# Moving the top-k penalty from VectorE's comparison to ScalarE's Sign in a fused attention and SwiGLU kernel

## The chip, the core and the metric

The kernel runs on one core of one Trainium2 chip. The metric is the device time of one execution in microseconds (us). In what follows PE is TensorE (PEld its weight load), DVE is VectorE, ACT is ScalarE, POOL is GpSimd, SP is SyncE, which issues most of the transfers.

## What is computed

Attention over 8 batches, 8 heads, 576 positions and 64 dimensions, in which each query keeps its 32 largest scores, followed by a SwiGLU block on the 4608 x 512 result:

```python
scores = scale * np.matmul(q, k.transpose(0, 1, 3, 2))
kth = np.partition(scores, -top_k, axis=-1)[..., -top_k:-top_k + 1]
scores = np.where(scores >= kth, scores, -1000000000.0)
scores = scores - np.max(scores, axis=-1, keepdims=True)
attn = np.exp(scores)
attn = attn / (np.sum(attn, axis=-1, keepdims=True) + 1e-09)
out = np.matmul(attn, v)
# x = out as (B*S, H*D)
g = x @ w_gate
silu = g * (1.0 / (1.0 + np.exp(-g)))
result = (silu * (x @ w_val)) @ w_out
```

The feed-forward width is 1536. All data are fp32.

## The kernel before

The work on attention is cut into 160 **units**: a batch, a tile of queries and a pair of heads. Of each batch's five tiles four have 128 queries (two heads side by side, 1152 score columns: a full unit), the last has 64 (both heads share the partitions, 576 columns). The feed-forward part is cut into 18 blocks of 256 rows of x, and each block into 36 **pieces** of four matmul calls; a call appears as two matmuls in the profile. The loop spreads pieces among the units. The weights are rounded once, in 72 pieces of 128x256, on ScalarE, GpSimd and VectorE, while the first units run.

The 32 largest of each row are found on VectorE in four rounds of eight; then VectorE compares the scores with the 32nd largest, and GpSimd adds the penalty:

```python
def select(n):
    ...
    e = work.tile([P, 2 * S], FP32, tag="e", name="e", bufs=4)
    for r in range(rounds):
        for t, hs in enumerate(heads):
            nc.vector.max(m[:, t, 8 * r : 8 * r + 8], cur[:, hs])          # L271
            yield
        if r < rounds - 1:
            for t, hs in enumerate(heads):
                nc.vector.match_replace(...)                               # L275
                yield
            cur = rest
    for t, hs in enumerate(heads):
        nc.vector.tensor_scalar(                                           # L281
            e[:, hs], sc[:, hs], m[:, t, TOP_K - 1 : TOP_K], FAR, ALU.is_lt, ALU.mult
        )

def penalize(n):
    nc.gpsimd.tensor_scalar_mul(bias[:, 0:nh], m[:, 0:nh, 0], -scale)      # L291
    nc.gpsimd.tensor_tensor(e[:, every], e[:, every], sc[:, every], ALU.add)   # L293

def weigh(n):           # ScalarE: Exp with the row sum                      L302
def normalize(n):       # GpSimd: + EPS L312; VectorE: reciprocal L314; ScalarE: scale L317
def turn(n):            # TensorE transposes e (L329), ScalarE copies the banks to et (L330)
def values(n):          # TensorE: et by v (L349, L358), ScalarE copies to xT (L373)
def scores(n):          # TensorE: L250 (L236 in the short tile), ScalarE copies to sc (L255, L241)
```

The score banks, the transposed banks, av and the banks of key and query preparation come from one pool of five PSUM tiles (`ps_t`); the products of the feed-forward block from another of three (`ps_f`).

A block of the feed-forward part; `need` drains the rounding of weights until those that the next product reads are there:

```python
def need(n):
    while ready[0] < n:
        next(weight)

def product(w, s, then):
    ps = ps_f.tile([P, 2, BLK], FP32, tag="f", name="f")
    need(8 * s + (4 if w is wg else 8))
    for i in range(2):
        m = 2 * s + i
        for kc in range(KC):
            nc.tensor.matmul(ps[:, i, :], w[:, kc, m * P : (m + 1) * P], x[:, kc, :], ...)  # L412
        if i == 1:
            on_act.append(lambda: then(ps))
        yield
# gate: Tanh (L430), half of g (L431), + 1 (L432) on ScalarE, then h * half on GpSimd (L433)
# value: copy on ScalarE (L437), then h * val on GpSimd (L438)
# output: matmuls of h by w_out (L449), copy on ScalarE (L460), store
```

One pass of the loop, cut:

```python
    flush(on_act)                     # ScalarE's part of the last products
    next(norm, None)                  # GpSimd: tot + EPS of unit n - 2
    penalize(n - 1)
    flush(on_pool)
    run(turn(n - TURN))               # TURN = 3
    finish_unit(n - VALUES)           # VALUES = 4
    next(nxt, None)                   # TensorE: scores of unit n + 1
    weigh(n - 1)                      # ScalarE: Exp of unit n - 1
    run(nxt)                          # ScalarE: copies to sc
    dve(2, beside=False)              # four steps of select(n)
    pieces(2); flush(on_act); flush(on_pool)
    dve(1); dve(1); next(norm, None); run(norm)
    next(ahead, None); pieces(1); next(ahead, None)
    dve(1); pieces(1); dve(2); run(topk); pieces(6)
```

`dve` also advances the rounding of the weights, about 4.5 of its pieces per full unit. Each engine runs its instructions in the order in which they are written here.

Of the kernel before, what the change touches and what calls it, by code (L numbers as in the profile page):

```python
# [8 lines left out]
AF = mybir.ActivationFunctionType  # L9
ALU = mybir.AluOpType  # L10
# [5 lines left out]
P = 128  # L16
TOP_K = 32
LOWEST = -3.4028234663852886e38
FAR = -3.0e38
EPS = 1.0e-9  # L20
BLK = 256
WP = 256
# [5 lines left out]
def kernel(  # L28
# [7 lines left out]
    w_out: bass.AP,  # L36
    out: bass.AP,
):

# [102 lines left out]
        for _ in range(n):  # L144
            next(weight, None)

    def need(n):

        while ready[0] < n:
            next(weight)  # L150

    pairs = [(b, hp) for b in range(B) for hp in range(NHP)]
    raw, preps = {}, {}
# [66 lines left out]
    def scores(n):  # L220
        b, qt, hp = units[n]
        slab = preps[b * NHP + hp]
        sc = work.tile([P, 2 * S], FP32, tag="sc", name="sc", bufs=2)
        halves = [slice(0, D), slice(D, P)]
        half = S // 2

        def bank():
            return ps_t.tile([P, 512], FP32, tag="t", name="s")


        if qt == J:
            banks = [bank() for _ in range(2)]
            for i, ps in enumerate(banks):
                for d in halves:
                    k0 = R + i * half
                    nc.tensor.matmul(  # L236
                        ps[d, 0:half], slab[d, S + R : S + 2 * R], slab[d, k0 : k0 + half]
                    )
            yield
            for i, ps in enumerate(banks):  # L240
                nc.scalar.copy(sc[:, i * half : (i + 1) * half], ps[:, 0:half])  # L241
        else:
            q0 = S + 2 * R + qt * P
            banks = []
            for i in range(2):
                for hh, d in enumerate(halves):
                    ps = bank()
                    banks.append((i + 2 * hh, ps))
                    k0 = (1 - hh) * R + i * half
                    nc.tensor.matmul(  # L250
                        ps[:, 0:half], slab[d, q0 : q0 + P], slab[d, k0 : k0 + half]
                    )
            yield
            for i, ps in banks:
                nc.scalar.copy(sc[:, i * half : (i + 1) * half], ps[:, 0:half])  # L255
        state[n] = dict(sc=sc)

    def select(n):

        nh = n_heads(units[n][1])  # L260
        sc = state[n]["sc"]
        m = small.tile([P, 2, TOP_K], FP32, tag="m", name="m", bufs=2)
        heads = [slice(t * S, (t + 1) * S) for t in range(nh)]
        rest = work.tile([P, 2 * S], FP32, tag="rest", name="rest", bufs=1)
        e = work.tile([P, 2 * S], FP32, tag="e", name="e", bufs=4)
        state[n] |= dict(m=m, e=e, heads=heads)
        cur = sc
        rounds = TOP_K // 8
        for r in range(rounds):
# [5 lines that stand above are left out]
                    nc.vector.match_replace(  # L275
                        rest[:, hs], m[:, t, 8 * r : 8 * r + 8], cur[:, hs], LOWEST
                    )
                    yield
                cur = rest
        for t, hs in enumerate(heads):  # L280
            nc.vector.tensor_scalar(  # L281
                e[:, hs], sc[:, hs], m[:, t, TOP_K - 1 : TOP_K], FAR, ALU.is_lt, ALU.mult
            )

    def penalize(n):

        st = state[n]
        sc, m, e, heads = st.pop("sc"), st.pop("m"), st["e"], st["heads"]
        nh = len(heads)
        bias = small.tile([P, 2], FP32, tag="bias", name="bias")  # L290
        nc.gpsimd.tensor_scalar_mul(bias[:, 0:nh], m[:, 0:nh, 0], -scale)  # L291
        every = slice(0, nh * S)
        nc.gpsimd.tensor_tensor(e[:, every], e[:, every], sc[:, every], ALU.add)  # L293
        st["bias"] = bias

    def weigh(n):

        st = state[n]
        e, heads, bias = st["e"], st["heads"], st.pop("bias")
        tot = small.tile([P, 2], FP32, tag="tot", name="tot")  # L300
        for t, hs in enumerate(heads):
            nc.scalar.activation(  # L302
                e[:, hs], e[:, hs], AF.Exp, bias=bias[:, t : t + 1], scale=scale,
                accum_out=tot[:, t : t + 1],
            )
        st["tot"] = tot
# [87 lines left out]
    def flush(queue):  # L394
        while queue:
            queue.pop(0)()

    def feed(kb):

        x = xT.pop(kb)
        hs = []

        def product(w, s, then):
            ps = ps_f.tile([P, 2, BLK], FP32, tag="f", name="f")
            need(8 * s + (4 if w is wg else 8))
            for i in range(2):
                m = 2 * s + i  # L410
                for kc in range(KC):
                    nc.tensor.matmul(  # L412
                        ps[:, i, :],
                        w[:, kc, m * P : (m + 1) * P],
                        x[:, kc, :],
                        start=(kc == 0),
                        stop=(kc == KC - 1),
                    )
                if i == 1:
                    on_act.append(lambda: then(ps))  # L420
                yield

        for s in range(MS):
            h = ffn.tile([P, 2, BLK], FP32, tag="h", name="h", bufs=MS + 1)
            hs.append(h)


            def gate(ps, h=h):
                half = ffn.tile([P, 2, BLK], FP32, tag="gv", name="half_g", bufs=3)
                nc.scalar.activation(h[:], ps[:], AF.Tanh, scale=0.5)  # L430
                nc.scalar.mul(half[:], ps[:], 0.5)  # L431
                nc.scalar.add(h[:], h[:], 1.0)  # L432
                on_pool.append(lambda: nc.gpsimd.tensor_mul(h[:], h[:], half[:]))  # L433

            def value(ps, h=h):
                val = ffn.tile([P, 2, BLK], FP32, tag="gv", name="val", bufs=3)
                nc.scalar.copy(val[:], ps[:])  # L437
                on_pool.append(lambda: nc.gpsimd.tensor_mul(h[:], h[:], val[:]))  # L438

            yield from product(wg, s, gate)  # L440
            yield from product(wv, s, value)
        for t in range(BLK // P):
            ps = ps_f.tile([P, DM], FP32, tag="f", name="o_ps")
            for m in range(MC):
                need(8 * MS + 2 * m + 2)
                if m == 6:
                    flush(on_act)
                    flush(on_pool)
                nc.tensor.matmul(  # L449
                    ps[:],  # L450
                    hs[m // 2][:, m % 2, t * P : (t + 1) * P],
                    wo[:, m, :],
                    start=(m == 0),
                    stop=(m == MC - 1),
                )
                if m == MC - 1:

                    def finish(ps=ps, t=t):
                        o = ffn.tile([P, DM], FP32, tag="o", name="o")
                        nc.scalar.copy(o[:], ps[:])  # L460
                        store(o, kb * BLK + t * P)

                    on_act.append(finish)
                if m % 2 == 1:
                    yield

    NU = len(units)
    todo = list(range(NBLK))
# [2 lines left out]
    def piece():  # L471

        if len(on_act) > 1:
            flush(on_act)
        if len(on_pool) > 1:
            flush(on_pool)
        while True:
            if not current:
                if not todo or done.get(todo[0], 0) < NHP * BLK:
                    return False  # L480
                flush(on_act)
                flush(on_pool)
                current.append(feed(todo.pop(0)))
            if next(current[0], 0) == 0:
                current.pop()
                continue
            return True

    def fetch(n):

# [5 lines left out]
            load(i + NHP)  # L496

    def pieces(n):
        for _ in range(n):
            if credit[0] >= 1 and piece():  # L500
                credit[0] -= 1

    def run(steps):
        for _ in steps:
# [19 lines left out]
    for n in range(NU + VALUES):  # L524
# [7 lines left out]
        def dve(k, beside=True):  # L532

            for _ in range(k * nh):
                next(topk, None)
                due[0] += 5 / 11 if beside else 0
                if due[0] >= 1:
                    due[0] -= 1
                    rounding(1)
# [11 lines left out]
            run(turn(n - TURN))  # L551
        if n >= VALUES:
            finish_unit(n - VALUES)
        next(nxt, None)
        if 0 <= n - 1 < NU:
            weigh(n - 1)
        run(nxt)

        dve(2, beside=False)
# [11 lines left out]
        next(ahead, None)  # L571
        pieces(1)
        next(ahead, None)
        dve(1)
        pieces(1)
        dve(2)
# [52 lines left out]
```

## Time and profile before

| what | value |
|---|---|
| median of 3 runs | 1914.77 us (1911.7 to 1914.82) |
| profiled run | 1915.14 us, span 1913.4 us |
| TensorE busy | 1756.5 us, 92% |
| VectorE busy | 1608.9 us, 84% |
| ScalarE busy | 1156.3 us, 60% |
| GpSimd busy | 816.0 us, 43% |
| mean granted TensorE clock | 0.959 |

The profile page gives the busy time of each engine, the span in 40 slices with the busy share in tenths, the chain of work that ended last, and the costliest groups of instructions with their mean duration and the idle time of the engine ahead of them. The clock row (PEclk) is what the throttle granted, in tenths of full speed. Busy times of TensorE include slow stretches at half clock, so its busy share has to be read together with that row.

### The profile page before, as it was taken

How to read it: one execution, taken by the hardware profiler on the slowest of the kernel's cores; microseconds unless marked ns; L12 is line 12 of the kernel's file. 1: busy time of each engine (PE TensorE's matmuls, PEld its weight loads, DVE VectorE, ACT ScalarE, POOL GpSimd, SP SyncE). 2: the span in 40 equal slices, each digit the busy share in tenths (PEclk: the TensorE clock that was granted, in tenths of full speed). 3: DMA queues.
4: the chain of work that ended last, by engine and by line, in shares of the span. 5: the costliest groups of instructions: out<-in, count | busy, mean ns of one | idle time of the engine just before them, and what ended most of it. 6: DMA issues, size and time to landing. Idle time of an engine off the chain costs nothing.

```text
span 1913.4 us, 29363 instructions
## 1 busy us (share of the span) xinstructions
PE 1756.5 (92%) x10144; PEld 1297.0 (68%) x10144; DVE 1608.9 (84%) x3476; ACT 1156.3 (60%) x2821; POOL 816.0 (43%) x846
## 2 busy tenths in 40 slices
PE   3437789989999999999999999999999999999999
PEld 2336558667677777676768676868686868586866
DVE  7999889998899979998799979999799989999400
ACT  5656656566666656675657566656675656665421
POOL 4566644335343525353335343525243535353412
PEclk7668899989999999999999999999999999999999
DMA  7322202000300012000210003000210001000000
GB/s 185 88 78 82 67 22 69 11 1 3 76 12 12 2 27 63 12 1 13 53 37 1 12 4 87 1 12 1 60 31 12 1 14 45 18 1 12 1 12 11
DMA packets 111253, 59.58 MB, mean 31 GB/s; under 512 B 89088, under 2 KB 97280, under 8 KB 111104
## 3 DMA queue, kind: packets, MB, share of 16 engines
q1 hardware_dynamic: 109904, 57.41, 11.5%
q8 instruction: 80, 1.31, 0.3%
q14 instruction: 69, 0.57, 0.1%
q10 hardware_dynamic: 1200, 0.30, 0.1%
HBM read 48.23 MB, written 9.44 MB: 30 GB/s over the span
## 4 chain that ended last, share of the span: by engine, by line
PE 82%; DVE 6%; POOL 5%; ACT 4%; issue 2%; DMA 0%; SPq 0%; POOLq 0%; DVEq 0%; ACTq 0%
PE f L412 38%; PE o_ps L449 19%; PE av L358 8%; PE etps L329 7%; PE s L250 7%; DVE m L271 2%; POOL e L293 2%; DVE rest L275 2%; PE s L236 2%; ACT e L302 1%; PE av L349 1%; PE kqps L205 1%; ACT sc L255 1%; POOL size L113 1%; POOL size L103 1%
## 5 line engine op out<-in xcount | busy, mean ns | idle before, releaser
L271 DVE MAX8 m<-rest 128x8 f32<-128x576 f32 x864 | 615.2, 747 | 2.2
L275 DVE MATCH_REPLACE8 rest<-m,rest 128x576 f32<-128x576 f32 x576 | 424.1, 743 | 0.0
L412 PE MATMUL f<-xT,wg 128*128 128x256 f32 x1728 | 407.5, 386 | 0.0
L293 POOL TENSOR_TENSOR e<-e,sc 128x1152 f32<-128x1152 f32 (+1 forms) x160 | 382.7, 2392 | 42.4 <-DVE e L281 38.8
L412 PE MATMUL f<-xT,wv 128*128 128x256 f32 x1728 | 395.8, 381 | 0.0
L449 PE MATMUL o_ps<-wo,h 128*128 128x512 f32 x864 | 387.6, 598 | 0.0
L412 PEld LDWEIGHTS f<-xT,wg 128*128 128x128 f32 x1728 | 324.2, 191 | 71.5 <-issue 29.9
L412 PEld LDWEIGHTS f<-xT,wv 128*128 128x128 f32 x1728 | 325.3, 190 | 53.3 <-issue 10.5
L433 POOL TENSOR_TENSOR h<-h,half_g 128x512 f32<-128x512 f32 x108 | 138.4, 1282 | 453.0 <-ACT h L432 435.0
L271 DVE MAX8 m<-sc 128x8 f32<-128x576 f32 x288 | 205.6, 750 | 123.9 <-ACT sc L255 78.8
L329 PE MATMUL etps<-ident,e 128*128 128x128 f32 (+1 forms) x1312 | 187.5, 288 | 125.9 <-POOL size L103 48.1
L449 PEld LDWEIGHTS o_ps<-wo,h 128*128 128x128 f32 x864 | 159.4, 190 | 193.1 <-issue 186.9
L329 PEld LDWEIGHTS etps<-ident,e 128*128 128x128 f32 (+1 forms) x1312 | 159.4, 147 | 176.1 <-POOL size L103 51.3
L330 ACT COPY et<-etps 128x512 f32<-128x512 f32 (+1 forms) x448 | 184.7, 482 | 148.5 <-PE etps L329 147.1
L302 ACT ACTIVATE e<-e,bias 128x576 f32<-128x576 f32 x288 | 222.1, 776 | 74.9 <-POOL e L293 74.5
L317 ACT ACTIVATE e<-e,tot 128x576 f32<-128x576 f32 x288 | 210.5, 780 | 5.4 <-DVE tot L314 5.1
L275 DVE MATCH_REPLACE8 rest<-m,sc 128x576 f32<-128x576 f32 x288 | 211.9, 742 | 0.0
L438 POOL TENSOR_TENSOR h<-h,val 128x512 f32<-128x512 f32 x108 | 139.7, 1293 | 149.6 <-ACT val L437 149.6
L250 PE MATMUL s<-kqT 64*128 64x288 f32 x1024 | 173.1, 446 | 9.6 <-ACT kqT L210 6.4
L312 POOL TENSOR_SCALAR tot<-tot 128x2 f32<-128x2 f32 (+1 forms) x160 | 37.4, 234 | 329.3 <-ACT e L302 320.9
L358 PE MATMUL av<-et,v 128*64 128x128 f32 (+1 forms) x2560 | 174.6, 282 | 0.0
L255 ACT COPY sc<-s 128x288 f32<-128x288 f32 x512 | 165.0, 410 | 2.5 <-PE s L250 2.5
(44 smaller groups left out, 1436.0 us busy)
## 6 DMA issues: line engine op xcount, KB each, us to landing
kq_in<-in_k_dram SPq DMA_DIRECT2D x64, 128.0 KB, 2.8
v<-in_v_dram SPq DMA_DIRECT2D x32, 256.0 KB, 3.0
kq_in<-in_q_dram SPq DMA_DIRECT2D x62, 128.0 KB, 3.1
w<-in_moe_w_gate_dram SPq DMA_DIRECT2D x24, 256.0 KB, 2.7
w<-in_moe_w_val_dram SPq DMA_DIRECT2D x24, 256.0 KB, 2.7
w<-in_moe_w_out_dram SPq DMA_DIRECT2D x24, 256.0 KB, 2.6
out_dram<-o SPq DMA_DIRECT2D x40, 128.0 KB, 2.4
out_dram<-o SPq DMA_DIRECT2D x16, 256.0 KB, 2.3
```

The costliest lines, as they stand in the source:

```text
L250: nc.tensor.matmul(ps[:, 0:half], slab[d, q0 : q0 + P], slab[d, k0 : k0 + half])
L255: nc.scalar.copy(sc[:, i * half : (i + 1) * half], ps[:, 0:half])
L271: nc.vector.max(m[:, t, 8 * r : 8 * r + 8], cur[:, hs])
L275: nc.vector.match_replace(rest[:, hs], m[:, t, 8 * r : 8 * r + 8], cur[:, hs], LOWEST)
L293: nc.gpsimd.tensor_tensor(e[:, every], e[:, every], sc[:, every], ALU.add)
L302: nc.scalar.activation(e[:, hs], e[:, hs], AF.Exp, bias=bias[:, t : t + 1], scale=scale, accum_out=tot[:, t : t + 1],)
L317: nc.scalar.mul(e[:, hs], e[:, hs], tot[:, t : t + 1])
L329: nc.tensor.transpose(ps[0:kl, c * P : (c + 1) * P], e[:, k0 : k0 + kl], ident[:])
L330: nc.scalar.copy(et[0:kl, c0 : c0 + cn, :], ps[0:kl, 0 : cn * P].rearrange("p (c j) -> p c j", c=cn),)
L358: nc.tensor.matmul(av[hh * R : (hh + 1) * R, 0:ql], v_last[:, hh, :] if c == J else vt[:, hh, c, :], moving, start=last and c == 0, stop=c ...
L412: nc.tensor.matmul(ps[:, i, :], w[:, kc, m * P : (m + 1) * P], x[:, kc, :], start=(kc == 0), stop=(kc == KC - 1),)
L449: nc.tensor.matmul(ps[:], hs[m // 2][:, m % 2, t * P : (t + 1) * P], wo[:, m, :], start=(m == 0), stop=(m == MC - 1),)
```

## The change

The comparison goes from VectorE. Instead ScalarE computes the sign of 2^30 x (score - 32nd largest), which is -1, 0 or 1; GpSimd takes the minimum with 0 and multiplies by 3e38, and adds the score, head by head. The negative of the 32nd largest, scaled, is made by a small GpSimd operation (`least`). This is meant to relieve VectorE, which in the first part of the kernel also rounds weights. Exp (`weigh`) moves from ahead of the score copies to after the normalization of the unit before. The tile e is taken in `penalize`, with three buffers instead of four; sc has three instead of two.

The first two feed-forward blocks are computed in halves of 128 rows, so that the first products can start when four units' values are there and not eight. And products no longer force the rounding of weights: where the weights are not there yet, the loop goes on without a piece.

```diff
-        for t, hs in enumerate(heads):
-            nc.vector.tensor_scalar(
-                e[:, hs], sc[:, hs], m[:, t, TOP_K - 1 : TOP_K], FAR, ALU.is_lt, ALU.mult
-            )
 
     def penalize(n):
...
+        e = work.tile([P, 2 * S], FP32, tag="e", name="e", bufs=3)
+        least = small.tile([P, 2], FP32, tag="least", name="least")
+        nc.gpsimd.tensor_scalar_mul(least[:, 0:nh], m[:, 0:nh, TOP_K - 1], -FINE)
         bias = small.tile([P, 2], FP32, tag="bias", name="bias")
         nc.gpsimd.tensor_scalar_mul(bias[:, 0:nh], m[:, 0:nh, 0], -scale)
-        every = slice(0, nh * S)
-        nc.gpsimd.tensor_tensor(e[:, every], e[:, every], sc[:, every], ALU.add)
-        st["bias"] = bias
+        for t, hs in enumerate(heads):
+            nc.scalar.activation(
+                e[:, hs], sc[:, hs], AF.Sign, bias=least[:, t : t + 1], scale=FINE
+            )
+            nc.gpsimd.tensor_scalar(e[:, hs], e[:, hs], 0.0, FAR, ALU.min, ALU.mult)
+            nc.gpsimd.tensor_tensor(e[:, hs], e[:, hs], sc[:, hs], ALU.add)
+        st |= dict(e=e, bias=bias)
...
-    def need(n):
+    def until(n):
         while ready[0] < n:
-            next(weight)
+            yield 0
...
+    def parts(kb):
+        return [slice(0, P), slice(P, BLK)] if kb < 2 else [slice(0, BLK)]
...
-        def product(w, s, then):
+        def product(w, s, c, then):
+            n = c.stop - c.start
+            yield from until(8 * s + (4 if w is wg else 8))
             ps = ps_f.tile([P, 2, BLK], FP32, tag="f", name="f")
-            need(8 * s + (4 if w is wg else 8))
...
-                        ps[:, i, :],
+                        ps[:, i, 0:n],
                         w[:, kc, m * P : (m + 1) * P],
-                        x[:, kc, :],
+                        x[:, kc, c],
...
-                yield
+                yield n / BLK
...
+        for c in parts(kb):
+            while done[kb] < NHP * c.stop:
+                yield 0
...
-        next(nxt, None)
-        if 0 <= n - 1 < NU:
-            weigh(n - 1)
         run(nxt)
...
         next(ahead, None)
         pieces(1)
         next(ahead, None)
+        if 0 <= n - 1 < NU:
+            weigh(n - 1)
         dve(1)
         pieces(1)
```

More of the change, by code (lines that the diff above doesn't have):

```diff
@@ L18 @@
 LOWEST = -3.4028234663852886e38
-FAR = -3.0e38
+FAR = 3.0e38
+FINE = 2.0**30
 EPS = 1.0e-9
@@ L222, in scores @@
         slab = preps[b * NHP + hp]
-        sc = work.tile([P, 2 * S], FP32, tag="sc", name="sc", bufs=2)
+        sc = work.tile([P, 2 * S], FP32, tag="sc", name="sc", bufs=3)
         halves = [slice(0, D), slice(D, P)]
@@ L264, in select @@
         rest = work.tile([P, 2 * S], FP32, tag="rest", name="rest", bufs=1)
-        e = work.tile([P, 2 * S], FP32, tag="e", name="e", bufs=4)
-        state[n] |= dict(m=m, e=e, heads=heads)
+        state[n] |= dict(m=m, heads=heads)
         cur = sc
@@ L279, in select @@
                 cur = rest
-        for t, hs in enumerate(heads):
-            nc.vector.tensor_scalar(
-                e[:, hs], sc[:, hs], m[:, t, TOP_K - 1 : TOP_K], FAR, ALU.is_lt, ALU.mult
-            )
     def penalize(n):
         st = state[n]
-        sc, m, e, heads = st.pop("sc"), st.pop("m"), st["e"], st["heads"]
+        sc, m, heads = st.pop("sc"), st.pop("m"), st["heads"]
         nh = len(heads)
+        e = work.tile([P, 2 * S], FP32, tag="e", name="e", bufs=3)
+        least = small.tile([P, 2], FP32, tag="least", name="least")
+        nc.gpsimd.tensor_scalar_mul(least[:, 0:nh], m[:, 0:nh, TOP_K - 1], -FINE)
         bias = small.tile([P, 2], FP32, tag="bias", name="bias")
         nc.gpsimd.tensor_scalar_mul(bias[:, 0:nh], m[:, 0:nh, 0], -scale)
-        every = slice(0, nh * S)
-        nc.gpsimd.tensor_tensor(e[:, every], e[:, every], sc[:, every], ALU.add)
-        st["bias"] = bias
+        for t, hs in enumerate(heads):
[5 more added lines that the diff above has]
+        st |= dict(e=e, bias=bias)
     def weigh(n):
@@ L396, in flush @@
             queue.pop(0)()
+    def parts(kb):
+        return [slice(0, P), slice(P, BLK)] if kb < 2 else [slice(0, BLK)]
     def feed(kb):
-        x = xT.pop(kb)
+        x = xT[kb]
         hs = []
-        def product(w, s, then):
+        def product(w, s, c, then):
+            n = c.stop - c.start
+            yield from until(8 * s + (4 if w is wg else 8))
             ps = ps_f.tile([P, 2, BLK], FP32, tag="f", name="f")
-            need(8 * s + (4 if w is wg else 8))
             for i in range(2):
@@ L419, in product, with gate, value @@
                 if i == 1:
-                    on_act.append(lambda: then(ps))
-                yield
[L423 to L441, printed above, removed]
+                    on_act.append(lambda: then(ps[:, :, 0:n], c))
+                yield n / BLK
+        for c in parts(kb):
+            while done[kb] < NHP * c.stop:
+                yield 0
+            for s in range(MS):
+                if c.start == 0:
+                    hs.append(ffn.tile([P, 2, BLK], FP32, tag="h", name="h", bufs=MS + 1))
+                h = hs[s]
+                def gate(ps, c, h=h):
+                    half = ffn.tile([P, 2, BLK], FP32, tag="gv", name="half_g", bufs=3)
+                    hc, gc = h[:, :, c], half[:, :, c]
+                    nc.scalar.activation(hc, ps, AF.Tanh, scale=0.5)
+                    nc.scalar.mul(gc, ps, 0.5)
+                    nc.scalar.add(hc, hc, 1.0)
+                    on_pool.append(lambda: nc.gpsimd.tensor_mul(hc, hc, gc))
+                def value(ps, c, h=h):
+                    val = ffn.tile([P, 2, BLK], FP32, tag="gv", name="val", bufs=3)
+                    hc, vc = h[:, :, c], val[:, :, c]
+                    nc.scalar.copy(vc, ps)
+                    on_pool.append(lambda: nc.gpsimd.tensor_mul(hc, hc, vc))
+                yield from product(wg, s, c, gate)
+                yield from product(wv, s, c, value)
+        del xT[kb]
         for t in range(BLK // P):
@@ L444, in feed @@
             for m in range(MC):
-                need(8 * MS + 2 * m + 2)
+                yield from until(8 * MS + 2 * m + 2)
                 if m == 6:
@@ L464, in feed @@
                 if m % 2 == 1:
-                    yield
+                    yield 1
     NU = len(units)
@@ L478, in piece @@
             if not current:
-                if not todo or done.get(todo[0], 0) < NHP * BLK:
-                    return False
+                if not todo or done.get(todo[0], 0) < NHP * parts(todo[0])[0].stop:
+                    return 0
                 flush(on_act)
@@ L483, in piece @@
                 current.append(feed(todo.pop(0)))
[L484 to L487, printed above, removed]
+            size = next(current[0], None)
+            if size is not None:
+                return size
+            current.pop()
     def fetch(n):
@@ L498, in pieces @@
     def pieces(n):
-        for _ in range(n):
-            if credit[0] >= 1 and piece():
-                credit[0] -= 1
+        while n > 0 and credit[0] >= 1:
+            size = piece()
+            if not size:
+                break
+            n -= size
+            credit[0] -= size
     def run(steps):
```

## The prediction

> **What bounds the kernel now.** I read the page from the top: the busy shares, then the slices with the granted clock, then the chain that ended last.
>
> ```profile
> PE 1756.5 (92%) x10144; PEld 1297.0 (68%) x10144; DVE 1608.9 (84%) x3476; ACT 1156.3 (60%) x2821; POOL 816.0 (43%) x846
> ...
> PE   3437789989999999999999999999999999999999
> ...
> PEclk7668899989999999999999999999999999999999
> ...
> PE 82%; DVE 6%; POOL 5%; ACT 4%; issue 2%; DMA 0%; SPq 0%; POOLq 0%; DVEq 0%; ACTq 0%
> ```
>
> 92% is an average over two different stretches: in the first slices TensorE is a third busy and its clock is low, from the tenth on it is full. The chain runs 82% on TensorE. So I asked for the busy time by stage (columns: us, then busy us of PE, its weight load, DVE, ACT, POOL; clock; DMA):
>
> ```profile
> 10.00:109.00 99.00, 38.96 (x208) 28.43 (x208) 92.07 (x219) 58.78 (x158) 53.95 (x78) 0.66 0.45 121
> 109.00:251.00 142.00, 96.56 (x517) 75.70 (x515) 123.90 (x286) 89.30 (x226) 88.66 (x119) 0.80 0.23 69
> 251.00:406.00 155.00, 142.19 (x837) 99.73 (x837) 144.48 (x309) 95.15 (x236) 59.34 (x61) 0.95 0.12 31
> 406.00:1812.00 1406.00, 1382.37 (x8167) 1028.26 (x8169) 1240.59 (x2646) 883.83 (x2140) 592.48 (x562) 1.00 0.08 21
> 1812.00:1913.00 101.00, 94.27 (x414) 63.09 (x410) 7.00 (x15) 25.16 (x54) 19.39 (x20) 0.96 0.05 11
> ```
>
> Up to 109 us VectorE sets the pace (92 of 99 us busy). From 406 to 1812 us TensorE is idle for 24 of 1406 us: there VectorE has 165 us to spare, and work taken from it is worth little. The last 101 us are TensorE alone.
>
> The added work sits on ScalarE, so I then looked for the place where TensorE depends on ScalarE within a unit. It is the banks: the pool of five holds three of transposed weights (etps), one of av and four of scores per full unit, so the second to fourth score banks are those that the copies to et (L330) have just emptied. Two units of the timeline:
>
> ```profile
> 592.12 0.59 ACT L460 COPY o<-o_ps 128x512 f32<-128x512 f32 x1 [5.63 <-PE o_ps L449]
> 592.60 1.25 ACT L330 COPY et<-etps 128x512 f32<-128x512 f32 x3
> 594.25 1.24 PE L250 MATMUL s<-kqT 64*128 64x288 f32 x8
> ...
> 638.74 0.63 ACT L432 ACTIVATE h<-h 128x512 f32<-128x512 f32 x1
> 639.26 1.24 ACT L330 COPY et<-etps 128x512 f32<-128x512 f32 x3
> 639.89 1.41 PE L250 MATMUL s<-kqT 64*128 64x288 f32 x8
> ```
>
> In the second unit the first et copy ends at about 639.85 and the scores start at 639.89: no slack. In the first there is about 1 us (copy done at 593.2, scores at 594.25). In the waits, `ACT et L330 <- PE etps` has 147.1 us in 70 units of 160: in those ScalarE itself is idle before the copy, 2.1 us on average.
>
> **What the Trainium skill says.** "TensorE: Matmul & The Clock Gate", Part 1: the array runs at half clock until it has been busy for some us. The trace agrees: between 50 and 140 us 128-column transposes follow each other every 213 ns, between 430 us and the end every 109 ns. "ScalarE: Activation LUTs", Table sets: functions of one set need no table load; the trace has one load in all (1.28 us) for Abs, Exp, Tanh and Copy. That Sign is in the same set no run here shows; if not, the two loads in each unit would be seen at once. "GPSIMD Engine Reference", Key points: it shares SBUF interfaces with VectorE. GpSimd's 128x256 scaling takes 0.40 us alone and 0.60 at times beside VectorE, which fits.
>
> **The change, part by part.** The durations are from groups of instructions by shape:
>
> ```profile
> L293 POOL TENSOR_TENSOR e<-e,sc 128x1152 f32<-128x1152 f32 x128 | 337.5, 2636 | 38.4 <-DVE e L281 34.8 <-PE etps L329 2.4
> L317 ACT ACTIVATE e<-e,tot 128x576 f32<-128x576 f32 x288 | 210.5, 780 | 5.4 <-DVE tot L314 5.1
> L281 DVE TENSOR_SCALAR e<-sc,m 128x576 f32<-128x576 f32 x288 | 146.9, 547 | 3.8 <-DVE m L271 0.5
> L293 POOL TENSOR_TENSOR e<-e,sc 128x576 f32<-128x576 f32 x32 | 45.2, 1412 | 4.0 <-DVE e L281 4.0
> L103 POOL TENSOR_SCALAR size<-size 128x256 f32<-128x256 f32 x72 | 32.2, 448 | 19.2 <-ACT size L101 18.6 <-POOL size L113 0.2
> ```
>
> (1) *VectorE* loses 288 comparisons: 147 us, 1.02 us per full unit. A full unit is 8 MAX8 and 6 MATCH_REPLACE8, about 10.57 us from unit to unit where nothing else holds it; it becomes 9.55.
>
> (2) *ScalarE* gains 288 Signs. L317 has the same shape: 780 ns alone, 1.44 us per pair in the timeline. 144 pairs by 1.45 is about 209 us: 1156 to about 1370.
>
> (3) *GpSimd* gains 288 clamps of 128x576. From L103 (0.40 us) and its two-element operations (0.22 us) 256 elements cost 0.18, so 576 cost about 0.22 + 0.41 = 0.63: 180 us. Adds split by head: 256 by 1.41 less 337 is 24. One small operation more per unit: 160 by 0.23 is 37. Sum about 241: 816 to about 1060. Per full unit about 5 us of 12: hidden.
>
> (4) *The start.* Nothing forced: the penalty adds of GpSimd, one per unit, start at 25.5, 40.3, 53.1, ... 138.7 us, 14.15 us apart; then, where the first block drains the rounding of weights, 15 to 18 apart, to 253.5. Now the rounding stays at 4.5 pieces per unit, and 1 us goes: about 13.2 each. The 16th add comes at about 24.5 + 15 x 13.2 = 223 instead of 253: 30 us earlier. The half blocks let TensorE begin after four units' values instead of eight. In the built order the first products stand with the ninth unit's scores, before with the thirteenth; up to the 17th unit's scores 29.5 pieces (1.75 us each in the timeline) are done, before 26. Halves cost TensorE nothing: 128-column steps follow at 109 ns, 256-column ones at 216. But from the 33rd unit on both orders are the same, piece for piece, and both leave the same 48 pieces to the end. Before it there are four units without any product where there were three: the 30 us survive, no more comes. Gain: 30.
>
> (5) *The steady stretch.* VectorE is the limit only where a block is not yet available (units 67, 111, 147 and a few): TensorE is idle there for 24 us in all, of which a faster VectorE returns perhaps a third. Gain: 8.
>
> (6) *The cost.* The new Signs stand on ScalarE ahead of the et copies, behind what is left of the last product. Where ScalarE was idle there for over 1.45 us they fit. Where it was not, the copies move by 1.45 us, and the scores, thus TensorE, by that less the slack. I went through the 128 units from the 33rd by their timeline. After a gate (h<-h), as at 638.7: about 1.8 us with the 0.1 of a wake-up, 14 units. After the key copies (kqT) 1.4 (12 units, some hidden). After a val copy without idle time about 1.0 (29 units), after an o copy 0.75 (10). In the others nothing or 0.2. From the 33rd unit on this is 75 us in 60 units. It repeats in each unit since ScalarE's last product work is tied to TensorE's. The move of Exp behind the score copies takes 1.94 us from the middle of the unit to its later part, which does not help the et copies.
>
> Not all will come: a stall before a unit in which TensorE waits anyway costs nothing, and an iteration's rest gives ScalarE time to catch up. I count 60 to 65 of the 75.
>
> Sum: 1914.8 - 30 - 8 + 63 = 1940.
>
> **The rivals.** *Everything hidden*: ScalarE at 1370 of some 1900 us is 72% busy, and busy shares alone say that it fits. Then parts 4 and 5 remain: about 1877. Against it is the 0.04 us of slack at 639.9. *The wait grows*: Sign waits for GpSimd's `least`, which stands behind products h*val of the unit before. Where those wait for ScalarE's last copy, 1.28 + 0.44 us come on top; in the built order they nearly always wait for an older one. Late products could also hold the output matmuls (L449), as GpSimd is in order and now spends 5 us on each penalty. Then 1980 or more. *VectorE was the bound*: then 147 us would come back, 1770. The 1382 of 1406 us speak against it.
>
> **Range and chances.** The start is good to 10 us, the stalls to 35: 1885 to 1990. Over 2% faster (below 1876) needs no stalls and a better start: 0.1. Over 2% slower (above 1953) needs the full count of stalls or the second rival: 0.35.
>
> **What will show it.** Step 1: VectorE at 1462 us, no L281. Steps 2, 3: Sign near 0.75 us, one table load, ScalarE 1370, GpSimd 1060. Step 4: the 16th penalty near 223 us. Step 6: score matmuls waiting for et copies, 60 us more idle time of TensorE after 406 us in pieces of 0.7 to 1.8 us; in the waits a row of et copies or scores behind Sign. I am wrong if TensorE is as full in the middle as now, or if the output matmuls wait for h.

## The result and the profile after

The changed kernel takes 2097.79 us (median of 5 runs, 2096.87 to 2098.65), the kernel before 1914.2 us beside it: a ratio of 1.0961, with a 95% interval of 1.0946 to 1.0976. It is 183 us slower, where 25 us were predicted; the measured time lies 108 us above the upper end of the range, 1990.

The page of the changed kernel, in the rows read before (busy us and share, the granted clock in 40 slices, the chain that ended last by engine):

```profile
PE 1850.3 (88%) x10528; PEld 1354.9 (65%) x10528; DVE 1481.6 (71%) x3188; ACT 1346.2 (64%) x3157; POOL 1476.6 (70%) x1446
...
PEclk7576879979999999999999999999999999999999
...
PE 57%; POOL 23%; ACT 10%; issue 5%; DVE 4%; DMA 0%; SPq 0%; POOLq 0%; ACTq 0%; DVEq 0%
```

VectorE and ScalarE are near the prediction (1462 and 1370). GpSimd is not: 1476.6 us instead of about 1060, and its share of the chain rose from 5% to 23%. The groups by line say which instruction it is (busy us, mean ns of one, idle time of the engine ahead of it):

```profile
L296 POOL TENSOR_SCALAR e<-e 128x576 f32<-128x576 f32 x288 | 618.6, 2148 | 200.1 <-ACT e L293 200.1
...
L297 POOL TENSOR_TENSOR e<-e,sc 128x576 f32<-128x576 f32 x288 | 405.6, 1408 | 24.0
...
L293 ACT ACTIVATE e<-sc,least 128x576 f32<-128x576 f32 x288 | 209.3, 770 | 98.6 <-POOL least L289 98.6
```

The clamp (L296) takes 2.148 us, not 0.63. The Sign (L293) takes what was expected. The table by stage, cut near the same places in the work as before (the last two cuts are the 33rd and the 160th unit's scores), with the same columns:

```profile
10.00:125.00 115.00, 44.14 (x206) 31.34 (x208) 87.30 (x206) 66.40 (x167) 79.58 (x101) 0.61 0.38 104
125.00:306.00 181.00, 117.60 (x727) 94.47 (x723) 117.60 (x279) 107.05 (x273) 136.00 (x172) 0.76 0.18 54
306.00:471.00 165.00, 145.84 (x1013) 108.15 (x1011) 130.94 (x279) 111.50 (x279) 116.03 (x118) 0.93 0.11 30
471.00:1992.00 1521.00, 1444.41 (x8169) 1054.76 (x8167) 1138.54 (x2411) 1030.13 (x2373) 1114.72 (x1022) 0.99 0.08 20
1992.00:2096.00 104.00, 96.16 (x422) 64.36 (x418) 6.33 (x14) 27.22 (x58) 28.12 (x26) 0.95 0.05 11
```

The 33rd unit's scores start at 471 instead of 406 us (65 us lost in the start), the steady stretch takes 1521 instead of 1406 (115 us), the tail 3 more. In the steady stretch TensorE's instructions are the same in number; it is idle for 77 us where it was idle for 24, and the busy time grew by 62. A unit there, in the timeline of all engines (start, us, engine and line; in brackets the idle time ahead and what ended it):

```profile
1870.64 1.44 ACT L293 ACTIVATE e<-sc,least 128x576 f32<-128x576 f32 x2 [0.18 <-POOL least L289]
1871.13 0.75 PE L252 MATMUL s<-kqT 64*128 64x288 f32 x2
1871.50 2.15 POOL L296 TENSOR_SCALAR e<-e 128x576 f32<-128x576 f32 x1 [0.70 <-ACT e L293]
1871.99 1.22 ACT L334 COPY et<-etps 128x512 f32<-128x512 f32 x3
1872.60 1.40 PE L252 MATMUL s<-kqT 64*128 64x288 f32 x6 [0.73 <-ACT et L334]
1873.73 1.41 POOL L297 TENSOR_TENSOR e<-e,sc 128x576 f32<-128x576 f32 x1
1875.10 2.14 POOL L296 TENSOR_SCALAR e<-e 128x576 f32<-128x576 f32 x1
```

This is step 6 of the prediction as it was described: two score matmuls run on the free bank at 1871.13, the other six wait until the two Signs are over and the first et copy has emptied the next bank (1872.60). The idle time is only 0.73 us. But the eight matmuls, 1.24 us in one group before, now take 0.75 + 1.40 = 2.15 us, since they no longer overlap: in that group of before they start two at a time, 0.01 us apart, and here one by one, at 1871.13 and 1871.47 us. Beside this GpSimd spends 7.1 us on the penalty of one unit.

The result therefore has at least two causes, the clamp and the order, besides what became of the start.

### The profile page after: what moved, and what is told of

It reads as the page before. It is cut to its first block, busy times and chain, and to the rows that moved or that the text cites. A ratio compares the mean times of both kernels' runs of the same rounds, so it can differ in the third digit from the quotient of the medians.

```text
span 2096.9 us, 30506 instructions
## 1 busy us (share of the span) xinstructions
PE 1850.3 (88%) x10528; PEld 1354.9 (65%) x10528; DVE 1481.6 (71%) x3188; ACT 1346.2 (64%) x3157; POOL 1476.6 (70%) x1446
## 4 chain that ended last, share of the span: by engine, by line
PE 57%; POOL 23%; ACT 10%; issue 5%; DVE 4%; DMA 0%; SPq 0%; POOLq 0%; ACTq 0%; DVEq 0%
PE f L421 28%; PE o_ps L465 14%; POOL e L296 10%; POOL e L297 6%; PE s L252 6%; ACT e L293 4%; PE etps L333 3%; PE av L362 3%; POOL h L447 2%; POOL h L453 2%; DVE m L272 2%; DVE rest L276 2%; PE s L238 1%; ACT et L334 1%; POOL size L115 1%
## 5 line engine op out<-in xcount | busy, mean ns | idle before, releaser
L296 POOL TENSOR_SCALAR e<-e 128x576 f32<-128x576 f32 x288 | 618.6, 2148 | 200.1 <-ACT e L293 200.1
L421 PE MATMUL f<-xT,wg 128*128 128x256 f32 (+1 forms) x1920 | 423.5, 372 | 7.1 <-DVE wg L118 7.1
L421 PE MATMUL f<-xT,wv 128*128 128x256 f32 (+1 forms) x1920 | 411.8, 367 | 16.2 <-DVE wv L118 8.5
L297 POOL TENSOR_TENSOR e<-e,sc 128x576 f32<-128x576 f32 x288 | 405.6, 1408 | 24.0
L252 PE MATMUL s<-kqT 64*128 64x288 f32 x1024 | 234.7, 474 | 100.5 <-ACT et L334 89.5
L293 ACT ACTIVATE e<-sc,least 128x576 f32<-128x576 f32 x288 | 209.3, 770 | 98.6 <-POOL least L289 98.6
L318 DVE RECIPROCAL tot<-tot 128x2 f32<-128x2 f32 (+1 forms) x160 | 26.1, 163 | 323.2 <-POOL tot L316 320.4
L252 PEld LDWEIGHTS s<-kqT 64*128 64x128 f32 x1024 | 122.1, 196 | 168.8 <-ACT et L334 131.3
L444 ACT ACTIVATE h<-f 128x512 f32<-128x512 f32 (+1 forms) x120 | 66.4, 553 | 215.2 <-PE f L421 215.1
L447 POOL TENSOR_TENSOR h<-h,half_g 128x512 f32<-128x512 f32 (+1 forms) x120 | 139.7, 1164 | 82.2 <-ACT h L446 80.4
```

What stands on the lines that cost most here:

```text
L252: nc.tensor.matmul(ps[:, 0:half], slab[d, q0 : q0 + P], slab[d, k0 : k0 + half])
L293: nc.scalar.activation(e[:, hs], sc[:, hs], AF.Sign, bias=least[:, t : t + 1], scale=FINE)
L296: nc.gpsimd.tensor_scalar(e[:, hs], e[:, hs], 0.0, FAR, ALU.min, ALU.mult)
L297: nc.gpsimd.tensor_tensor(e[:, hs], e[:, hs], sc[:, hs], ALU.add)
L421: nc.tensor.matmul(ps[:, i, 0:n], w[:, kc, m * P : (m + 1) * P], x[:, kc, c], start=(kc == 0), stop=(kc == KC - 1),)
L447: on_pool.append(lambda: nc.gpsimd.tensor_mul(hc, hc, gc))
```

## The experiments

Ratios are to the kernel before, run beside each. "33rd scores" is the start of the 33rd unit's scores in the profiled run (406 us before), "steady stretch" is from there to the 160th unit's scores (1406 us before). The letters of the theories are those of the texts on record.

**The operation by itself.** To the end of the kernel before 13 elementwise operations were added, three of each: twelve on GpSimd, one after the other, and one on VectorE, which runs beside GpSimd's first.

```diff
+ gpsimd.tensor_scalar(dst, own, 0.0, 3e38, min, mult)     # also on other data, with
+ gpsimd.tensor_scalar(dst, own, 0.0, 1.0, min, max)       # another constant, swapped,
+ gpsimd.tensor_scalar(dst, own, -1.0, 1.5e38, add, mult)  # one operation alone, 256 wide
```

> The kernel before, with three repeats each of thirteen elementwise operations appended after the last output, when no other engine computes. It measures GpSimd's cost of the clamp by itself. Theory A (the pair of operations is slow on GpSimd): minimum followed by multiplication on 128x576 takes about 2.15 us here too, with any constant and any data, while minimum followed by maximum takes 0.6 to 0.7 us. Rival B (contention with VectorE, which is always busy in the changed kernel): alone, the clamp takes 0.6 to 0.7 us like the other pairs. Rival C (the constant 3e38 or the values -1, 0, 1 make it slow): with the constant 2, or on random weights, it takes 0.6 to 0.7 us.

GpSimd's timeline there (start, then the time of all three):

```profile
1908.65 6.87 POOL L593 TENSOR_SCALAR dst<-own 128x576 f32<-128x576 f32 x3 [20.29 <-ACT own L589]
...
1935.54 2.16 POOL L601 TENSOR_SCALAR dst<-own 128x576 f32<-128x576 f32 x3
1937.79 2.18 POOL L603 TENSOR_SCALAR dst<-own 128x576 f32<-128x576 f32 x3
1940.05 5.11 POOL L605 TENSOR_SCALAR dst<-own 128x576 f32<-128x576 f32 x3
```

L593 is the clamp, minimum then product. The first of the three runs beside VectorE's operations and takes 2.42 us; from the second on no other engine computes, and one takes 2.13 to 2.15 us. L601, minimum then maximum, takes 0.667, and L603, sum then product, 0.671. L605, one product alone, takes 1.65. Other data (L595), the constant 2.0 in place of 3e38 (L597) and the swapped pair (L599) made no difference (2.13 us). So theory A holds: the pair of operations sets the time, not contention and not the values. VectorE did the same clamp in 0.573 us on the mean of three (0.46, 0.80 and 0.46).

**One half of the change at a time.** First only the penalty, with the feed of the feed-forward part as before; then only the halves and the unforced weights, with the penalty as before.

```diff
# only the penalty
-    vector.tensor_scalar(e, sc, kth, FAR, is_lt, mult); gpsimd e + sc
+    scalar Sign; gpsimd min, mult; gpsimd + sc; Exp moved as in the change
# only the feed
+    parts(kb): halves for kb < 2; until() in place of need()
```

> The kernel before with only the penalty changed (Sign, clamp, add by head, the later Exp, the buffers); whole blocks and forced rounding as before. Theory A (the clamp's 2.15 us on GpSimd, and Sign's place on ScalarE, are the loss): 2090 to 2150 us, as slow as the changed kernel or slower. Rival D (the halves and the unforced rounding make the loss): 1910 to 1960 us.

> The kernel before with only the halves of the first two blocks and the unforced rounding; comparison on VectorE and one add on GpSimd as before. Theory A with part 4 of the prediction, less the 1 us per unit of VectorE: the start gets 10 to 20 us shorter, 1895 to 1905 us. Rival D: 2000 us or more.

Only the penalty: 2100.75 us, ratio 1.0982 (1.0966 to 1.0998). All of the loss is there, in the penalty together with the later Exp and the buffers. Only the feed: 1921.72 us, ratio 1.0045 (1.0028 to 1.0062), where 10 to 20 us were expected to be gained. The 33rd scores came at 414.8 us, 9 later. The same products took TensorE 99.7 us up to there instead of 89.2. TensorE in its timeline:

```profile
116.09 2.05 PE L418 MATMUL f<-xT,wv 128*128 128x128 f32 x16 [1.20 <-ACT half_g L442]
117.98 1.95 PE L418 MATMUL f<-xT,wg 128*128 128x128 f32 x16
125.30 3.78 PE L418 MATMUL f<-xT,wv 128*128 128x128 f32 x16 [5.37 <-ACT half_g L442]
```

When the first half block becomes available, the credit of pieces saved up until then is spent at once: from the ninth unit's scores to the tenth's it is 26.9 us (14.1 before), and TensorE waits 5.37 us for ScalarE to take a product out of its bank. VectorE, which sets the pace up to here, waits as well: its eighth and ninth unit take 17.6 and 19.5 us instead of 14.8 and 13.6.

**No clamp.** In place of the sign ScalarE makes the penalty in one step, Relu of 2^100 x (32nd largest - score), and GpSimd subtracts it in one wide operation. All else is as in the change.

```diff
- scalar.activation(e, sc, Sign, bias=least, scale=FINE)
- gpsimd.tensor_scalar(e, e, 0.0, FAR, min, mult); gpsimd.tensor_tensor(e, e, sc, add)   # per head
+ scalar.activation(e, sc, Relu, bias=BIG * kth, scale=-BIG)                             # BIG = 2.0**100
+ gpsimd.tensor_tensor(e[:, every], sc[:, every], e[:, every], subtract)
```

> The changed kernel without the clamp: ScalarE computes Relu of 2^100 x (32nd largest - score) in Sign's place, and GpSimd subtracts it from the score in one operation per unit, as wide as the add of before. Same result. ScalarE's work and order stay. Theory A with step 6 of the prediction (Sign ahead of the et copies costs about 60 us, the rest of the 183 us is the clamp): near 1940 us, the figure predicted with a cheap clamp. Rival E (the place of Sign on ScalarE is the whole loss): above 2030 us. Rival F (only the clamp matters, ScalarE's order costs nothing): 1870 to 1890 us.

2019.89 us, ratio 1.056 (1.0543 to 1.0577), between theory A's figure and theory E's. By the ratios 77 us come back without the clamp and 107 remain, so the clamp is not the whole loss. The score matmuls of the steady stretch (128-query units only, 430 to 1919 us; busy us, mean ns, idle ahead) against those of the kernel before (406 to 1812 us):

```profile
L250 PE MATMUL s<-kqT 64*128 64x288 f32 x800 | 127.1, 432 | 0.1
```

```profile
L252 PE MATMUL s<-kqT 64*128 64x288 f32 x800 | 164.5, 448 | 32.4 <-ACT et L334 32.4
```

The same 800 matmuls take 37 us more and are waited for 32 us more, all of it for et copies. With the short units' 8 us this is 78 of the 83 us that the steady stretch is longer. So the Relu in the Sign's place costs it, without any clamp.

**Another form for the clamp.** Sum then product, and the bias of the sign one step of precision lower so that a score equal to the 32nd largest still gives +1; everything else is the change.

```diff
- gpsimd.tensor_scalar(e, e, 0.0, FAR, min, mult)
+ gpsimd.tensor_scalar(e, e, -1.0, 1.5e38, add, mult)
- least = kth * -FINE
+ least = kth * (-FINE * (1.0 - 2.0**-24))
```

> The changed kernel with one difference: the clamp (minimum with 0, times 3e38) becomes (minus 1, times 1.5e38), a pair that took 0.67 us alone where the old one took 2.13; the 32nd largest in Sign's bias is lowered by one unit in the last place, so that it counts as positive. Order, operation count and everything else stay. Theory A (the clamp was mis-sized by 1.5 us, 288 times, on the chain of GpSimd): what the Relu variant has, 2005 to 2035 us, so about 75 us of the 183 are the clamp's duration. Rival F (the clamp is the whole loss): under 1960 us. Rival E (its duration does not matter): over 2080 us.

2022.61 us, ratio 1.0566 (1.055 to 1.0582); the operation takes 0.675 us:

```profile
L296 POOL TENSOR_SCALAR e<-e 128x576 f32<-128x576 f32 x288 | 194.4, 675 | 230.0 <-ACT e L293 219.2
```

Sign with this pair and Relu without any cost the same. The slow pair alone is worth 75 us, 39 of it in the start (33rd scores at 432.3 instead of 471.4) and 32 in the steady stretch. In the start VectorE's share of the rounding, the shift of the weight sizes, stands behind GpSimd's limiting of the same tile, and GpSimd is in order. VectorE's waits for it (us in all, times, longest) in the kernel before, in the change and here:

```profile
DVE size L110 <- POOL size L103: 28.5, 16, 6.2
...
DVE size L112 <- POOL size L105: 95.1, 25, 10.8
...
DVE size L112 <- POOL size L105: 45.9, 28, 7.8
```

In the steady stretch Sign waited for `least` 62.0 us in the change, at most 2.3 at once, and 37.1 here.

**The order on ScalarE.** The penalty of the unit goes behind the copies to et and xT: with the slow clamp, with Relu, and with Relu behind the score copies too.

```diff
     next(norm, None)
-    penalize(n - 1)
     flush(on_pool); run(turn(n - TURN)); finish_unit(n - VALUES)
+    penalize(n - 1)          # the third kernel: behind run(nxt)
     next(nxt, None); ...; run(nxt)
```

> The changed kernel with its slow clamp, but Sign, clamp and add stand behind the transposes' copies (et) and the xT copies of the same pass, ahead of the score copies. Theory E (ScalarE waits in Sign while TensorE waits for the et copies behind it): most of the waits of the scores for et (45.7 us of idle TensorE after the 33rd unit, more as slower issue) go; 2020 to 2060 us. Rival G (GpSimd is so full with 7 us of penalty per unit that the order on ScalarE does not matter): 2085 us or more.

> The Relu variant (no clamp) with Relu behind the et and xT copies, ahead of the score copies. Theory E: the 83 us that the Relu variant loses between the 33rd and the 160th unit's scores are its place ahead of the et copies; they fall to under 20, total 1935 to 1955 us. Rival H (they come from ScalarE's amount of work or from the later Exp): total over 1990 us.

> The Relu variant with Relu behind the score copies too. VectorE then gets its next scores first. Theory E: as with Relu behind the et copies, 1930 to 1955 us, a few us less where VectorE waited for scores. Rival H: over 1990 us.

Sign: 2048.49 us (ratio 1.0694, 1.0677 to 1.0711). Relu: 1934.05 us (1.0102, 1.0087 to 1.0117). Relu last: 1949.47 us (1.0183, 1.0166 to 1.02). The score matmuls with Relu late, in the same stretch (419 to 1828 us):

```profile
L252 PE MATMUL s<-kqT 64*128 64x288 f32 x800 | 130.4, 435 | 0.5 <-ACT et L334 0.3
```

One move, with ScalarE's work the same, gives back 88 us by the ratios. The waits for et copies are gone and the steady stretch is 1409 us, near the 1406 of before. The move also puts GpSimd's part of the penalty behind its products of h. But TensorE did not wait for these: no such wait is listed for the steady stretch with Relu early, and one of 0.8 us in the change. Half clock fell with the waits for et copies, from 31.5 us of this stretch with Relu early to 11.3 (11.7 before; 42.3 in the change). Last is 15 us worse than late: the 33rd scores come at 431.7 instead of 419.0 us, in the start.

The two costs don't simply add. Against Relu, Sign with the slow clamp costs 77 us in the order of the change and 113 in the late order. The early order costs 88 us with Relu and 51 with the slow clamp.

**The feed again, with the late Relu.** Whole blocks and forced weights as before, so that only the penalty differs from the kernel before.

```diff
- parts(kb): halves for kb < 2; until()
+ whole blocks; need()
```

> Relu behind the et copies as before, but with the kernel before's feed: whole blocks and forced rounding. What it differs in from the kernel before is the penalty alone. Theory J (the start of the Relu kernels gains nothing because the last step of the weights' rounding on VectorE, which has two inputs, is held up to 2.6 us while GpSimd's two-input subtraction runs): units two to eight stay about 14.2 us apart and the start ends about where before's does; halves and unforced rounding cost 5 to 10 us, as they did alone, so 1915 to 1930 us. Rival K (the halves are what cancels the gain of the start): units 13.2 us apart, 1885 to 1900 us.

1911.39 us, ratio 0.9984 (0.9978 to 0.9991). Here the halves with the unforced weights had cost 23 us, where theory J expected 5 to 10. The later Exp and the changed buffers are in this kernel too, so the loss is not theirs. But 288 comparisons fewer on VectorE bring 3 us: in the profiled runs the 33rd scores come 11 us earlier (394.7), and the steady stretch and the tail are 6 and 2 us longer. The first units, in which VectorE sets the pace, gain nothing: from the third to the eighth VectorE's unit is 14.31 us, 14.12 before. Its timeline with GpSimd's (both in one answer) shows why:

```profile
71.13 2.62 POOL L295 TENSOR_TENSOR e<-sc,e 128x1152 f32<-128x1152 f32 x1 [1.26 <-ACT e L292]
71.76 2.27 DVE L116 SCALAR_TENSOR_TENSOR wg<-w,size 128x256 int32<-128x256 int32 x1
73.95 0.28 DVE L110 TENSOR_SCALAR size<-size 128x256 int32<-128x256 int32 x1
```

L116, the last step of the rounding, takes 0.41 us as a rule (the median). Here it starts inside GpSimd's subtraction and ends 0.28 us after it, at 74.03. In the kernel before the longest of these 72 was 2.44 us and their sum 33.6; here 14 are over 0.9 us and the sum is 50.6.

**Is it the number of inputs, or the length of GpSimd's operation?** Three kernels from the last one. The first does the rounding's last step with one input; it leaves out the sign of the weights. The second subtracts head by head. The third is the kernel before with whole blocks, only unforced.

```diff
# one input
- vector.scalar_tensor_tensor(out=dst, in0=high, scalar=-0x40000000, in1=bits, op0=and, op1=or)
+ vector.tensor_scalar(dst, bits, -1, 0, and, or)
# per head
- gpsimd.tensor_tensor(e[:, every], sc[:, every], e[:, every], subtract)
+ for hs in heads: gpsimd.tensor_tensor(e[:, hs], sc[:, hs], e[:, hs], subtract)
# the kernel before
- need(n)
+ yield from until(n)
```

> The same kernel, but the last step of the weights' rounding reads one input: it copies the rounded bits and leaves the sign out, so the weights are their absolute values (the output is not the reference's). Theory J: the holding-up goes; units two to eight 12.3 to 13.3 us apart (1.9 us of blocking and 0.4 of shorter operations less), and the total is 15 to 30 us under the run with two inputs. Rival L (VectorE waits for GpSimd by semaphores, not for its inputs): within 8 us of it, which the shorter operation alone explains.

> Relu behind the et copies, whole blocks, forced rounding, two inputs; GpSimd subtracts head by head, two operations of about 1.4 us in place of one of 2.63. Theory J: a weight operation is held up for at most 1.4 us and the first begins earlier, so units two to eight 13.2 to 13.8 us apart and the total 5 to 15 us under the unsplit one. Rival L: the same or 1 to 3 us slower for the additional operation.

> The kernel before with only the unforced rounding (whole blocks, comparison on VectorE). It splits the 10 us that halves and unforced rounding lost together. If halves carry it: 1905 to 1915 us, no slower than before. If the missing force carries it (products then wait for weights that VectorE makes late in the same pass): 1920 us or more.

One input: 1904.76 us, ratio 0.9956 (0.9938 to 0.9973), a gain of 6.6 where 15 to 30 were expected. The step still took up to 2.17 us, in 14 places, so two inputs are not what makes it wait. Per head: 1905.94 us, 0.9957 (0.9943 to 0.9972). VectorE's unit falls from 14.31 to 13.66 us:

```profile
68.56 2.98 POOL L295 TENSOR_TENSOR e<-sc,e 128x576 f32<-128x576 f32 x2 [0.60 <-ACT e L291]
69.86 0.40 DVE L116 SCALAR_TENSOR_TENSOR wg<-w,size 128x256 int32<-128x256 int32 x1
70.19 1.50 DVE L110 TENSOR_SCALAR size<-size 128x256 int32<-128x256 int32 x1
```

Now at most one operation of 1.4 to 1.6 us is waited for: L110 takes up to 1.50 us, L116 up to 1.62, and the 72 of L116 sum to 36.5 us. Unforced alone: 1914.27 us, 0.9998 (0.9989 to 1.0007), nothing. So with the comparison on VectorE the halves carry the feed's loss; behind the late Relu the two were not taken apart.

**Halves without the burst; and a better place.** The credit of pieces is capped at 3 up to the 17th unit, in the kernel with only the feed. The last kernel is the one with the subtraction per head, with one more step of `select` early in the pass and one fewer later, so that VectorE's roundings fall elsewhere.

```diff
# halves, paced
- credit[0] = min(credit[0] + ..., 8.0)
+ credit[0] = min(credit[0] + ..., 3.0 if n < 17 else 8.0)
# shifted
- dve(2, beside=False) ... dve(1) ...    due[0] += 5 / 11
+ dve(3, beside=False) ...               due[0] += 5 / 9
```

> The kernel with halves and unforced rounding alone (comparison on VectorE, which lost 10 us), with its products in the first 17 units held to about 2.5 pieces per unit, without the bursts of 7.5 pieces in the 9th and 13th unit. Theory M (the bursts put products ahead of the weights' rounding in ScalarE's and GpSimd's order, and VectorE, which bounds the start, waits): the 33rd unit's scores come at 400 to 408 us in place of 414.8, total 1905 to 1915 us. Rival N (it is the halves' greater number of instructions, or their waits on weights made in the same pass): 1918 us or more.

> The fastest so far (whole blocks, forced rounding, Relu behind the et copies, subtraction by head, 1906 us), with the weights' rounding begun two VectorE steps later in each unit and then at a higher rate, so that no weight operation meets GpSimd's subtraction. Theory J (a scaling or merging operation of VectorE is held while GpSimd's two-input operation runs): units two to eight from 13.66 to about 12.6 us apart, total 1890 to 1902 us. Rival L: no gain, 1905 us or more, since the rounding's steps then wait for each other.

Paced halves: 1917.63 us, ratio 1.0018 (1.0011 to 1.0025). This lies between the two theories: the burst explains about 5 of the 8.6 us, and the rest stays open. Shifted: 1897.45 us, ratio **0.9917 (0.9896 to 0.9937)**, with VectorE's unit at 13.44 us, still not the 12.6 expected. This beats both kernels:

```profile
PE 1763.9 (93%) x10144; PEld 1299.5 (69%) x10144; DVE 1479.1 (78%) x3188; ACT 1333.2 (70%) x3109; POOL 863.3 (46%) x1134
```

ScalarE is as loaded as in the changed kernel (1346 us there), VectorE too. What is different is where the operations stand, which form GpSimd's have, and that the blocks are whole again.

## Why the prediction was wrong

One path from the kernel before to the changed one, by the ratios times 1914 us:

| step | us |
|---|---|
| penalty by Relu, behind the et and xT copies | -3 |
| halves and unforced weights | +23 |
| penalty ahead of the et copies | +88 |
| Sign with sum and product in place of Relu | +1 |
| minimum and product in place of sum and product | +75 |
| sum | +184 |

Since the costs don't add, another path would split the 184 us otherwise; with the slow clamp in place halves and unforced weights cost nothing (2100.75 us without them, 2097.79 with them).

**Step 3 failed, and it is the largest error.** "So 576 cost about 0.22 + 0.41 = 0.63" was scaled up from a different operation: L103 took 0.40 us for 256 elements, and it is a minimum and a maximum. For that pair the scaling was good (0.667 us at 576). The clamp has another pair of operations and takes 2.148 us. GpSimd's penalty is then 7.1 us per unit instead of 5, and "hidden" failed as well: 75 us. The pair of sum and product, measured in its place at 0.675 us, would have cost about what the estimate said. The Trainium skill ("GPSIMD Engine Reference", 4.1 Engine selection) calls elementwise work with one input roughly line-rate on GpSimd; the measurement decides against it for this pair, 2.13 us against VectorE's mean of 0.573, while for sum and product, 0.671, it is not far off.

**Step 4 failed with the wrong sign.** The start was to gain 30 us; with the fast form of the clamp it lost 26 (33rd scores at 432.3 us), with the slow one 65. The 16th penalty's add came at 306 us, not at 223. By the 33rd scores of the profiled runs, along the path of the table: Relu, late, -11 us; halves and unforced weights +24; ahead of the et copies +11; Sign with sum and product +2.5; the slow pair +39.

Three terms were wrong. The pace of 13.2 us took the comparison's 1.02 us off and left the rest as it was. From the third to the eighth unit VectorE took 17.04 us in the changed kernel, with its shifts waiting for GpSimd behind the clamp. With the fast pair it was 14.48, with Relu 14.31, since the last steps of the rounding were held beside GpSimd's operations on two tensors (up to 1.46 us with the fast pair, up to 2.29 with Relu late and whole blocks), and 13.66 with the late subtraction cut in two. In the changed kernel itself no last step took over 0.89 us. "Halves cost TensorE nothing" failed too: the same products took 99.7 us instead of 89.2 up to the 33rd scores (93.4 when paced), and their burst held up the unit loop. Up to there VectorE is the busier engine, 361 of 406 us before against TensorE's 280, so TensorE's work moved ahead brought nothing that the runs show. And the penalty ahead of the et copies cost 11 us here too (Relu early against late).

**Step 6 was right in kind and too small.** The place, the reason and the size of one stall were as described: with Relu early, 44 waits of up to 1.6 us for et copies. 63 us were predicted, 80 measured in the steady stretch (Relu early against late), and with step 5's gain of 8 not there the stretch is 83 longer than before. "60 us more idle time" was not what the trace showed: only 35 of the 80 us are idle time of TensorE, and 45 sit in longer busy time. The discount from 75 to 63 for stalls that cost nothing was not borne out. Half clock rose by 20 us with the order, for which the count had no term; half of it, 10 us, is an estimate of what that cost.

**Step 5** brought nothing: the steady stretch takes 1412 us with whole blocks and late Relu, against 1406. **Steps 1 and 2** held. VectorE lost 127 us of busy time, not 147: the comparison overlapped its neighbours, as the sum of the groups before (1752 us) exceeds the busy time of 1609. It went from 10.57 to 9.70 us from unit to unit, near the 9.55 predicted. Sign took 770 ns, ScalarE 1346 us.

That functions of one set need no further table load, as the Trainium skill says ("ScalarE: Activation LUTs", Table sets), fits: the changed kernel has one load in all, of 1.283 us, and so have the kernels with Relu, so Sign and Relu are used beside Exp and Tanh without another.

Of the rivals "the wait grows" came nearest in its number, and partly in its reason: Sign did wait for `least`, 98.6 us in all. But most of the loss in order needs no such wait: with Relu it was 32.4 us in the steady stretch, at most 0.6 at once, and the stalls of up to 1.6 us were there all the same. The other half of that rival, output matmuls waiting for h, hardly came: one wait of 0.8 us in the steady stretch. With step 3 put right (the kernel with sum and product, 2022.61 us) the prediction would still have been some 84 us too low, by the positions in the profiled runs: 56 in the start, 28 in the steady stretch.

Open are the last 3 us of the halves with the comparison, why the steady stretch is 6 us longer with the late Relu and whole blocks, why the halves cost 23 us behind the late Relu and 8 with the comparison, and how the slow clamp lengthens the steady stretch in detail: more waits for `least`, more half clock (24.3 to 42.3 us) and longer score waits (at most 3.5 us instead of 1.6) go with it, but were not separated.

## What to carry to other kernels

Take the time of an operation from a row with the same pair of operations, not only the same engine, shape and type; where there is none, measure it alone first. In this case an engine that was busy for two thirds of the time still cost 88 us, since new work was put ahead of the copy that frees a bank another engine waits for. Look for the place in its queue where the work has slack, before counting its busy time. Work taken from the engine that sets the pace brought only what its neighbours left: look at whether its other instructions get longer.

## What the runs showed of the hardware

- GpSimd, 128x576 fp32, with no other engine computing: minimum and maximum 0.667 us, sum and product 0.671, minimum and product 2.13, product alone 1.65, minimum alone 1.645, sum or product of two tensors 1.395. For minimum and product neither the data nor the constants tried made a difference.
- Beside GpSimd's operation on two tensors VectorE's integer steps on 128x256 (0.28 to 0.41 us) can last until about 0.3 us after that operation, up to 2.81 us beside one of 2.63 us. The Trainium skill ("GPSIMD Engine Reference", Key points) names VectorE instructions in a 2-port mode or with two SBUF inputs for such contention; the one-input step was held for up to 2.17 us all the same. Which mode it ran in no run here shows. MAX8 and MATCH_REPLACE8 on 128x576 were not held: they kept their mean of 0.74 to 0.75 us.
- Eight score matmuls in one group, started two at a time, took 1.24 us; in groups of two and six they took 2.15 us without the wait between them.
